# Longformer attention and a token and channel mixer on one core: interleaved queries for heads 4 to 7 of batch 0, mask rows behind adds, moved loads, and the last output tile in halves

## The chip, the cores and the metric

The kernel runs on one core of a Trainium2 chip. The metric is the device time of one execution in microseconds (us). Before the change the median of 5 runs is 309.93 us (307.6 to 310.61). All times below are in us from the start of the profiled span, unless they are durations.

## The reference, cut to what matters

For each of 8 batches and 8 heads, attention over 576 positions of 64 channels, with a mask: a query sees the keys within 32 positions, 8 global positions see and are seen by all. The result, as `x` of 576 x 512 per batch, goes through two dense layers along the positions and two along the channels.

```python
scores = scale * np.matmul(q, k.transpose(0, 1, 3, 2))
mask = np.abs(pos[:, None] - pos[None, :]) <= 32
mask = mask | is_global[:, None] | is_global[None, :]
attn = softmax(np.where(mask, scores, -1e9))          # along the keys
x = np.matmul(attn, v)                                # (8, 576, 512) after joining the heads
h = np.maximum(x.transpose(0, 2, 1) @ w_tok1, 0.0) @ w_tok2
u = x + h.transpose(0, 2, 1)
out = u + np.maximum(u @ w_ch1, 0.0) @ w_ch2
```

## The kernel before, in words

**Tiles.** A batch's 576 positions are five tiles (`tau`) of 128; the last holds 64. Only the band of the scores is computed. A head's band lies in the free dimension of `e_all` (`e0` for batch 0) in five blocks; the scores come as a "part 0" and a "part 1" for four heads (`hg`, 0 or 1), two heads to a PSUM tile.

**Work of one batch**, by the names in the profile:
- `load_qk`, `load_v`: loads on GpSimd's queue. `Xk`, `Xq`: transposes of k and q on VectorE (into `kc`, `qc`). `Kc`, `Xc`: GpSimd copies of these into `kT`, `qT`, where each tile's positions are interleaved with the 8 globals; `globals_`, `globals_k` (VectorE or GpSimd) write the globals there. `dup_v` is one copy `vsh<-vsh` on SP's queue, after the v loads.
- `S_step`: scores `s` of a `hg` and part; ScalarE takes the exponentials (L343). `S_mask`: VectorE multiplies a head's row of `e_all` by the band (L362), in pairs of heads 0, 1 and 2, 3 of the `hg`. `S_eg`: GpSimd copies the global columns into `eg`.
- `OG`: the rows of the global queries (`og`). `PV`: attention times v for a tile (`pv`), with two matmuls a head, and `norm` on VectorE.
- `M1` (`a1p`, then ScalarE), `M2` (`hp`, then VectorE adds `x` into `u`, and for the last 64 rows into `ul`), `M3`: SP's transposing DMA `uT<-u` (parts 0 and 1) and, in odd batches, `uTl<-ul`, since the last 64 rows of two batches are done together.
- `M4` (12 times: `b1p`, L492, then ScalarE), `M4l` (`b1lp`, L505, odd batches), `M5` (`op`, L518, four parts of three matmuls a tile; VectorE adds `u` into `osb`, L522 or L525; SP stores it).

**PSUM.** Pool `psm` has two one-bank buffers for `M4` and `M5`, `psS` two two-bank buffers (scores and others), `psV` one (all of `M2`, among others). A buffer is reused when its reader is done.

**Order.** Each round b of the loop merges two lists by their costs: first D4 (`M4` and `M4l` of batch b) with `OG`, `PV` and `M1` of batch b+1 and the transposes of batch b+2; then D5 (`M5` of batch b) with `M2` of b+1 and the scores of b+2. `run` calls a unit; `later(n, f)` calls f when n units, the present one among them, have run. So VectorE's queue has its masks after a fixed number of units (L562 to L569). Each engine runs its queue in order, and so do the DMA queues of GpSimd and SP. In a round D5 of even b, VectorE has: masks of heads 0, 1; masks of heads 2, 3; the `u` add of `M2` part 1; `osb`; `ul`; and for the second `hg`: masks 0, 1; `osb`; masks 2, 3; `osb`.

**Batch 0.** It is written out by hand (L730 on), heads 0 to 3 ahead of 4 to 7, in a buffer `e0` that lies where later `b1` and `wc2` do. Its scores (`S_nat`, L295) read the queries from `qc` and the globals apart, so that a segment is cut into pieces: 36 score matmuls a tile for part 0 and 32 for part 1, after the bias matmuls that add the mask (L298). `S_tile` (L315) does the same with 16 from the interleaved `qT`; batch 1 uses it. `fillt` issues matmuls on zeros that nobody reads.

Of the kernel before, what the change touches and what calls it, by code (L numbers as in the profile page):

```python
# [45 lines left out]
LAG_PV = 1  # L46
TDMA = 1
NEG = -20000.0
FILL = (33, 2, 0, 0)


@with_exitstack
def kernel(
# [31 lines left out]
    def pss(shape, dtype=F32, name="s"):  # L85
        return psS.tile(shape, dtype, tag="s", name=name)
# [93 lines left out]
    q16s = [halves(t) for t in qTs]  # L180
    qcs = [const.tile([P, NT * P], I32, name=f"qc{i}") for i in range(2)]
    kcs = [const.tile([P, NT * P], I32, name=f"kc{i}") for i in range(2)]
    e_all = const.tile([P, H, EW], F16)
    big = const.tile([P, 2, NJ, 512], F16)
    b1, wc2 = big[:, 0], big[:, 1]
    e0 = big.rearrange("p a j x -> p (a j x)")[:, 0 : H * EW].rearrange("p (h x) -> p h x", h=H)
# [125 lines left out]
                        )  # L312
        S_exp(b, hg, part, rp, ps)

    def S_tile(b, hg, part, rp, bias):  # L315
        ps = pss([P, 2, 512], name=f"s_{b}_{hg}_{part}_{rp}")
        qf, kT = q16s[b % 2][:, hg], k16s[b % 2][:, hg]
        if bias:
            for i in range(2):
                for off, c0, n in B_SEG[part]:  # L320
                    nc.tensor.matmul(
                        ps[:, i, off : off + n], lhsT=identS, rhs=biasm[:, c0 : c0 + n], start=(off == 0), stop=False,
                    )
        for off, kc, lo, n in S_SEG[part]:
            for e in range(2):
                for i in range(2):
                    r = 2 * rp + i
                    rs = slice(32 * r, 32 * r + 32)
                    nc.tensor.matmul(
                        ps[:, i, off : off + n], lhsT=kT[rs, kc : kc + P, e], rhs=qf[rs, lo : lo + n, e],  # L330
                        start=(e == 0 and not bias), stop=(e == 1 and (off == S_SEG[part][-1][0] or not bias)),
                    )
        S_exp(b, hg, part, rp, ps)
# [63 lines left out]
    def PV(b, tau, get):  # L397
        s = st[b]
        ps = get([P, 2, 512], name=f"pv_{b}_{tau}")
        odd_last = tau == NT - 1 and b % 2 == 1  # L400
        sh = 64 if odd_last else 0
        x16, vs = x16s[b % 2], vsh[b % 2]
        e = e_all if b else e0
        for hf in range(2):
            for hh in range(4):
                h = 4 * hf + hh
                o = ps[:, hf, VW * hh : VW * hh + VW]
                c0 = EB * tau + NG - sh
                m = 64 if tau == NT - 1 and not sh else P
                nc.tensor.matmul(o[0:m], lhsT=e[:, h, c0 : c0 + m], rhs=vs[:, tau, h, :], start=True, stop=(tau == NT - 1))  # L410
                if tau < NT - 1:
                    c1 = EB * tau + 136 + (NG if tau == 0 else 0)
                    nc.tensor.matmul(  # L413
                        o, lhsT=e[:, h, c1 : c1 + P], rhs=vs[:, NT - 1 + tau if tau else 1, h, :], start=False, stop=True
                    )

        def norm():
            r = slice(0, P) if tau < NT - 1 else slice(sh, sh + 64)
            pq = ps[:, :, 0 : 4 * VW].rearrange("p f (h x) -> p f h x", h=4)
            rr = tiny.tile([P, 2, 4], F32, tag="rr", name=f"rr_{b}_{tau}")  # L420
            nc.vector.reciprocal(out=rr[r], in_=pq[r, :, :, D])  # L421
            nc.vector.tensor_tensor(  # L422
                out=x16[r, tau, :].rearrange("p (f h x) -> p f h x", f=2, h=4), in0=pq[r, :, :, 0:D],
                in1=rr[r].unsqueeze(3).to_broadcast([P if tau < NT - 1 else 64, 2, 4, D]), op=ALU.mult,
            )
        return norm
# [83 lines left out]

    def M5(b, tau, part):
        s = st[b]
        if part == 0:
            s["o"] = psm([P, 512], name=f"op_{b}_{tau}")
        ps = s["o"]
# [45 lines left out]
    def u_S(b, hg, part):  # L561
        def f():  # L562
            S_step(b, hg, part)
            if part:
                later(LAG_S, lambda: S_mask(b, hg, (0, 1)))
                later(LAG_S + (5 if hg else 1), lambda: S_mask(b, hg, (2, 3)))
                later(LAG_S + (6 if hg else 2), lambda: S_eg(b, hg))
        return f

    def u_PV(b, tau, get):  # L570
# [327 lines left out]
    Xq(0, 1)  # L898
    Xv0(0)
    glob0(1)  # L900
    Xv0(1)
    S_nat(0, 0, 1, 0, psv, True)
    S_nat(0, 0, 1, 1, pss, True)
    load_v(0, (5, 6, 7), False)
    nc.gpsimd.dma_start(out=w1, in_=moe_w_tok1[0 : S - LAST, :].rearrange("(c p) x -> p c x", p=P))
    for i in range(2):
        nc.gpsimd.dma_start(out=w1l[64 * i : 64 * i + LAST, i], in_=moe_w_tok1[S - LAST : S, :])
# [6 lines left out]
    eg_const(1, nc.gpsimd.tensor_copy)  # L914
    nc.gpsimd.memset(vsh[1][32:64, NT:NC, :, 0:D], 0.0)
    load_v(1, (2, 3, 4), False)
    S_nat(0, 1, 0, 0, pss, True)
    S_nat(0, 1, 0, 1, psv, True)
    shift_v(0)
    nc.vector.memset(e0[:, 0:4, 200:208], 0.0)  # L920
    S_eg(0, 0)
# [9 lines left out]
    s0["uT"] = mb.tile([P, 4, 4, P], F16, tag="uT", name="uT_0")  # L931

    og = psm([P, 512], name="og0")
    OGh(0, og)
    S_nat(0, 1, 1, 0, pss, True)
    S_nat(0, 1, 1, 1, pss, True)
    zero_e(e_all)
    rfh(0, og)
    p01 = psv([P, 2, 512], name="pv0_01")
    fillt(p01[:, 1], FILL[2])  # L940
    PVh(0, PAIRS[0], p01)
    p23 = pss([P, 2, 512], name="pv0_23")
    PVh(0, PAIRS[1], p23)
# [109 lines left out]
    for b in range(B):  # L1053
        D4, D5 = dense(b)
        if b == 0:
# [21 lines left out]
            load_qk(3)  # L1077
            gather(gq, q, 1)
            gather(gk, k, 1)
            load_v(3)  # L1080
        else:
            A, Bs = [], []
            if b + 1 < B:
# [5 lines left out]
                A = G(b + 2) + A[:4] + weave(A[4:], X_units(b + 2))  # L1089
                Bs = mix(Bs, phase_s(b + 2))  # L1090
            if b + 3 < B:
                A = A[:2] + zero(lambda: load_qk(b + 3)) + A[2:]
                Bs = Bs[:5] + zero(lambda: load_v(b + 3)) + Bs[5:]
            merge(A, D4)
            merge(Bs, D5)
# [31 lines left out]
```

## Time and profile before

| | |
|---|---|
| median of 5 runs | 309.93 us |
| the 5 runs | 307.6, 309.93, 308.28, 309.98, 310.61 |
| the profiled execution | 308.04 us, of which the span is 306.2 |
| TensorE clock granted | 0.998 |
| idle before matmuls, all places | 13.4 (span less PE busy) |
| POOL waits for the masks, before `eg` copies (L368) | 66.9 in 12 places |
| SP waits for v loads, before `vsh<-vsh` (L130) | 99.2 in 8 places |
| round 0, D5 | about 57.4 to 73.6 |
| round 2, D5; round 4, D5 | about 126.5 to 142.2; 194.6 to 210.2 |
| scores of batch 3, first tile | 93.99 |
| last matmul starts, last add, last stores issued | 301.2, 301.58, 302.29 |

A timeline line holds the start, the duration, the engine, the line of the kernel, the operation with output and inputs, its shape, how many instructions are merged in it, and in brackets the idle time before it and what ended that. PE is TensorE's matmuls, PEld its weight loads, DVE VectorE, ACT ScalarE, POOL GpSimd, SP the queue that issues stores. A matmul of 512 columns has a duration of about 0.38 in its row, but they follow each other every 0.2155, since they are pipelined.

### The profile page before, as it was taken

To read this page: it belongs to the slowest core of one execution; us is meant where nothing else is said; L and a number is where in the kernel's file an instruction comes from. 1 tells how busy PE (TensorE), PEld (TensorE's weight loads), DVE (VectorE), ACT (ScalarE), POOL (GpSimd) and SP (SyncE) were. 2 spreads that over 40 slices of the span, in tenths; PEclk is the share of its full clock that TensorE was granted. 3 is DMA by queue.
4 is the path that set the end of the run, shared out by engine and by line. 5 is a ranking of instruction groups with operands and counts; after the bars stand their busy time and mean duration, and the time that the engine had idled before them with its cause. 6 is when DMAs were issued, how large, how long until landed. Compare 5 with 4: busy or idle time off the path is not lost.

```text
span 306.2 us, 8076 instructions
## 1 busy us (share of the span) xinstructions
PE 292.8 (96%) x3349; PEld 158.1 (52%) x3349; DVE 189.8 (62%) x369; ACT 156.9 (51%) x320; POOL 112.8 (37%) x212
## 2 busy tenths in 40 slices
PE   8998899899999999999999999999999999999993
PEld 3677565444565446444565446444564445444641
DVE  8877869785592767595582867585674865240021
ACT  7986795463545625654546524554455535206500
POOL 7898591332884560327140651326040000000000
PEclk9999999999999999999999999999999999999999
DMA  7999999996999699029941699049402320061022
GB/s 114 143 113 205 192 141 195 111 112 188 169 87 188 115 121 253 27 72 145 179 106 28 102 130 254 7 96 120 128 2 68 106 71 0 2 171 52 3 100 71
DMA packets 69381, 34.34 MB, mean 112 GB/s; under 512 B 55968, under 2 KB 59936, under 8 KB 69344
## 3 DMA queue, kind: packets, MB, share of 16 engines
q0 software_dynamic: 44960, 18.19, 50.6%
q1 hardware_dynamic: 24384, 15.63, 19.1%
q8 instruction: 26, 0.43, 0.6%
q14 instruction: 11, 0.09, 0.1%
HBM read 36.38 MB, written 9.44 MB: 150 GB/s over the span
## 4 chain that ended last, share of the span: by engine, by line
PE 63%; DVE 7%; POOL 3%; DMA 3%; issue 2%; ACT 1%; DVEq 0%; POOLq 0%; ACTq 0%
PE op L518 24%; PE b1p L492 20%; DVE e_all L362 5%; PE hp L451 4%; PE s L286 4%; PE a1p L435 4%; DMA q<-in_q_dram 3%; PE b1lp L505 3%; PE pv L410 2%; PE pv L413 2%; ACT e_all L343 1%; DVE u L456 1%; DVE osb L522 1%; POOL vsh L125 1%; PE og L378 1%
## 5 line engine op out<-in xcount | busy, mean ns | idle before, releaser
L719 ACT ACTIVATE big<-b1p 128x512 f16<-128x512 f32 x96 | 57.6, 602 | 79.1 <-PE b1p L492 79.1
L492 PE MATMUL b1p<-uT,wc 128*128 128x512 f16 x376 | 91.3, 379 | 1.5 <-DVE osb L522 1.5
L518 PE MATMUL op<-big 128*128 128x512 f16 x384 | 91.8, 380 | 0.0
L343 ACT ACTIVATE e_all<-s 128x544 f16<-128x544 f32 (+3 forms) x140 | 59.0, 522 | 32.5 <-PE s L286 30.6
L518 PEld LDWEIGHTS <-big 128*128 128x128 f16 x384 | 35.5, 98 | 40.5
L492 PEld LDWEIGHTS <-wc 128*128 128x128 f16 x376 | 33.5, 97 | 38.3 <-issue 4.8
L362 DVE TENSOR_TENSOR e_all<-e_all,bandm 128x1160 f16<-128x1160 f16 x54 | 38.1, 757 | 15.8 <-ACT e_all L343 15.8
L125 POOL DMA_DIRECT2D vsh<-in_v_dram x60 | 41.9, 711 | 3.7 <-DMA gq<-in_q_dram,idx_i 1.4
L456 DVE TENSOR_TENSOR u<-x,hp 128x1024 f16<-128x1024 f16 x14 | 17.0, 1217 | 31.8 <-PE hp L451 31.8
L522 DVE TENSOR_TENSOR osb<-u,op 128x512 f32<-128x512 f16 x32 | 21.9, 683 | 24.0 <-PE op L518 23.7
L368 POOL COPY eg<-e_all 128x160 f16<-128x160 f16 (+1 forms) x24 | 6.4, 295 | 66.9 <-DVE e_all L362 66.9
L253 POOL COPY kT<-kc 128x640 int32<-128x640 int32 x15 | 10.9, 724 | 48.1 <-DVE rr L421 35.0
L422 DVE TENSOR_TENSOR x<-pv,rr 128x512 f16<-128x512 f32 (+1 forms) x35 | 24.2, 691 | 1.4
L410 PEld LDWEIGHTS <-e_all 128*128 128x128 f16 (+1 forms) x280 | 17.9, 98 | 5.9 <-issue 1.5
L410 PE MATMUL pv<-vsh,e_all 128*128 128x66 f16 (+1 forms) x280 | 20.0, 194 | 0.2 <-DVE x L422 0.2
L451 PE MATMUL hp<-a,w 128*128 128x512 f16 x72 | 19.1, 379 | 0.8 <-DVE u L456 0.8
L240 DVE STREAM_TRANSPOSE kc<-k 128x576 int32<-128x576 int32 x16 | 19.9, 1243 | 0.1
L246 DVE STREAM_TRANSPOSE qc<-q 128x576 int32<-128x576 int32 x16 | 19.8, 1235 | 0.0
L286 PEld LDWEIGHTS <-kT 32*128 32x128 f16 x768 | 12.0, 92 | 11.3 <-issue 10.0
L413 PE MATMUL pv<-vsh,e_all 128*128 128x66 f16 x224 | 17.0, 193 | 0.1
L384 DVE TENSOR_TENSOR vsh<-og,dsel 32x132 f16<-32x132 f32 x28 | 8.1, 288 | 13.4 <-PE og L378 12.9
L286 PE MATMUL s<-qT,kT 32*128 32x104 f16 (+3 forms) x768 | 15.4, 214 | 1.0 <-POOL qT L253 0.6
(161 smaller groups left out, 323.6 us busy)
## 6 DMA issues: line engine op xcount, KB each, us to landing
out_dram<-osb SPq DMA_DIRECT2D x32, 256.0 KB, 2.4
k<-in_k_dram POOLq DMA_DIRECT2D x16, 288.0 KB, 5.9
q<-in_q_dram POOLq DMA_DIRECT2D x16, 288.0 KB, 8.3
vsh<-in_v_dram POOLq DMA_DIRECT2D x36, 96.0 KB, 5.4
vsh<-vsh SPq DMA_DIRECT2D x6, 297.0 KB, 5.8
wc<-in_moe_w_ch_dram POOLq DMA_DIRECT2D x3, 512.0 KB, 13.8
big<-in_moe_w_ch_dram POOLq DMA_DIRECT2D x3, 512.0 KB, 10.3
out_dram<-osb SPq DMA_DIRECT2D x8, 128.0 KB, 5.9
```

Of the source, the lines that this page charges most:

```text
L125: nc.gpsimd.dma_start(out=V[p0:p1, c, :, 0:D], in_=v[b, :, j0 : j0 + p1 - p0, :].rearrange("h p d -> p h d"))
L286: nc.tensor.matmul(tiles[r // 2][:, r % 2, off : off + n], lhsT=kT[rs, kc : kc + P, e], rhs=qf[rs, lo : lo + n, e], start=(e == 0), stop=( ...
L343: nc.scalar.activation(out=o, in_=i, func=AF.Exp, scale=scale)
L362: nc.vector.tensor_mul(out=eh, in0=eh, in1=bandm)
L410: nc.tensor.matmul(o[0:m], lhsT=e[:, h, c0 : c0 + m], rhs=vs[:, tau, h, :], start=True, stop=(tau == NT - 1))
L413: nc.tensor.matmul(o, lhsT=e[:, h, c1 : c1 + P], rhs=vs[:, NT - 1 + tau if tau else 1, h, :], start=False, stop=True)
L422: nc.vector.tensor_tensor(out=x16[r, tau, :].rearrange("p (f h x) -> p f h x", f=2, h=4), in0=pq[r, :, :, 0:D], in1=rr[r].unsqueeze(3).to_ ...
L451: nc.tensor.matmul(ps[:, i, :], lhsT=w2[:, ch, P * tau - sh : P * tau - sh + P], rhs=s["a1"][:, ch, :], start=(ch == 0), stop=(ch == 1),)
L492: nc.tensor.matmul(ps, lhsT=wc1[:, cc, P * j : P * j + P], rhs=s["uT"][:, :, cc, :], start=(cc == 0), stop=(cc == 3))
L518: nc.tensor.matmul(ps, lhsT=w, rhs=wc2[:, j, :], start=(j == 0), stop=(j == NJ - 1))
L522: nc.vector.tensor_add(out=osb, in0=s["u16"][:, tau], in1=ps)
L719: nc.scalar.activation(out=st[b]["b1"][:, j, :], in_=ps, func=AF.Relu)
```

## The change

1. **Start.** Heads 4 to 7 of batch 0 take their scores with `S_tile` instead of `S_nat`. For that `globals_` of these heads is done on VectorE and `Xc` on GpSimd, ahead of the weight loads. The tile of part 1, heads 4 and 5, moves ahead of `OGh(0)`; two fillers that write `og` stand between them.
2. **v of the last tile.** In even batches the last `pv` tile takes 128 columns of `e_all` where it took 64. The rows beyond are not read later. For the last head 64 columns are added behind `e_all` and zeroed on ScalarE.
3. **Masks.** The masks of heads 2, 3 and the `eg` copies come one unit later.
4. **Loads.** `load_v(3)` moves from the end of round 0 to round 1, behind the first two copies of globals for batch 3, where `load_qk(4)` stood; that one goes to the end of the first list.
5. **Last output tile.** Its `M5` is done in two halves of 256 columns, each in its own PSUM buffer, with its own add; the stores of the two batches' rows leave on SP's and ScalarE's queues.

```diff
-FILL = (33, 2, 0, 0)
+FILL = (33, 2, 2, 0)
...
-    e_all = const.tile([P, H, EW], F16)
+    e_pad = const.tile([P, H * EW + 64], F16, name="e_all")
+    e_all = e_pad[:, 0 : H * EW].rearrange("p (h x) -> p h x", h=H)
...
-    def S_tile(b, hg, part, rp, bias):
-        ps = pss([P, 2, 512], name=f"s_{b}_{hg}_{part}_{rp}")
+    def S_tile(b, hg, part, rp, bias, get=pss):
+        ps = get([P, 2, 512], name=f"s_{b}_{hg}_{part}_{rp}")
...
-                m = 64 if tau == NT - 1 and not sh else P
-                nc.tensor.matmul(o[0:m], lhsT=e[:, h, c0 : c0 + m], rhs=vs[:, tau, h, :], start=True, stop=(tau == NT - 1))
+                nc.tensor.matmul(o, lhsT=e_pad[:, EW * h + c0 : EW * h + c0 + P], rhs=vs[:, tau, h, :], start=True, stop=(tau == NT - 1))
...
+        if b == B - 1 and tau == NT - 1:
+            if part:
+                return
+            osb = ob.tile([P, DM], F32, tag="osb", name=f"osb_{b}_{tau}")
+            for c in range(2):
+                x = slice(256 * c, 256 * c + 256)
+                ps = psm([P, 256], name=f"op_{b}_{tau}_{c}")
+                for j in range(NJ):
+                    nc.tensor.matmul(ps, lhsT=s["b1l"][:, j, :], rhs=wc2[:, j, x], start=(j == 0), stop=(j == NJ - 1))
+                nc.vector.tensor_add(out=osb[:, x], in0=s["ul"][:, x], in1=ps)
+                for i, eng in enumerate((nc.sync, nc.scalar)):
+                    eng.dma_start(out=out[b - 1 + i, S - LAST : S, x], in_=osb[64 * i : 64 * i + 64, x])
+            return
...
-                later(LAG_S + (5 if hg else 1), lambda: S_mask(b, hg, (2, 3)))
-                later(LAG_S + (6 if hg else 2), lambda: S_eg(b, hg))
+                later(LAG_S + (6 if hg else 2), lambda: S_mask(b, hg, (2, 3)))
+                later(LAG_S + (7 if hg else 3), lambda: S_eg(b, hg))
...
     glob0(1)
+    globals_(0, nc.vector, (1,))
     Xv0(1)
...
     load_v(0, (5, 6, 7), False)
+    Xc(0, 1, nc.gpsimd)
     nc.gpsimd.dma_start(out=w1, in_=moe_w_tok1[0 : S - LAST, :].rearrange("(c p) x -> p c x", p=P))
...
-    S_nat(0, 1, 0, 0, pss, True)
-    S_nat(0, 1, 0, 1, psv, True)
+    S_tile(0, 1, 0, 0, True, pss)
+    S_tile(0, 1, 0, 1, True, psv)
...
     og = psm([P, 512], name="og0")
+    S_tile(0, 1, 1, 0, True, pss)
+    fillt(og, FILL[2])
     OGh(0, og)
-    S_nat(0, 1, 1, 0, pss, True)
-    S_nat(0, 1, 1, 1, pss, True)
+    S_tile(0, 1, 1, 1, True, pss)
     zero_e(e_all)
+    zeros(e_pad[:, H * EW :])
...
-    fillt(p01[:, 1], FILL[2])
...
-            load_v(3)
...
-                A = A[:2] + zero(lambda: load_qk(b + 3)) + A[2:]
+                if b == 1:
+                    A = A[:2] + zero(lambda: load_v(3)) + A[2:] + zero(lambda: load_qk(4))
+                else:
+                    A = A[:2] + zero(lambda: load_qk(b + 3)) + A[2:]
```

More of the change, by code (lines that the diff above doesn't have):

```diff
@@ L402, in PV @@
         x16, vs = x16s[b % 2], vsh[b % 2]
-        e = e_all if b else e0
+        e = e_all
         for hf in range(2):
```

## The prediction

> **What bounds the kernel now.** I read the page first, then TensorE's own waits, then the timeline at each place that the change touches.
>
> ```profile
> span 306.2 us, 8076 instructions
> PE 292.8 (96%) x3349; PEld 158.1 (52%) x3349; DVE 189.8 (62%) x369; ACT 156.9 (51%) x320; POOL 112.8 (37%) x212
> ```
>
> TensorE is busy 96% of the span and no other engine over 62%: only TensorE's 13.4 us of idle time, its own work, and the time after its last matmul can shrink. Its waits, with total, count and longest in us:
>
> ```profile
> PE b1p L492 <- DVE osb L522: 1.5, 3, 0.5
> ...
> PE a1p L660 <- DVE x L651: 0.9, 2, 0.7
> PE hp L451 <- DVE u L456: 0.8, 3, 0.3
> ...
> PE s L286 <- POOL qT L253: 0.6, 1, 0.6
> PE s L286 <- ACT a L438: 0.4, 1, 0.4
> ```
>
> Two come three times, in the dense second halves of rounds 0, 2 and 4. The timeline of round 0 (start, duration, engine, line) shows them; the other two rounds look alike:
>
> ```profile
> 66.29 1.47 PE L518 MATMUL op<-big 128*128 128x512 f16 x6
> 66.73 1.21 DVE L456 TENSOR_TENSOR u<-x,hp 128x1024 f16<-128x1024 f16 x1
> 68.00 0.59 PE L451 MATMUL hp<-a,w 128*128 128x512 f16 x2 [0.23 <-DVE u L456]
> 73.02 1.43 DVE L362 TENSOR_TENSOR e_all<-e_all,bandm 128x1160 f16<-128x1160 f16 x2
> 73.61 1.03 PE L492 MATMUL b1p<-uT,wc 128*128 128x512 f16 x4
> 74.36 0.68 DVE L522 TENSOR_TENSOR osb<-u,op 128x512 f32<-128x512 f16 x1
> 75.09 1.89 PE L492 MATMUL b1p<-uT,wc 128*128 128x512 f16 x8 [0.46 <-DVE osb L522]
> ```
>
> The adds that free a PSUM buffer stand behind two mask multiplies. One more place matters, the transpose of the odd batch's last rows (`uTl`) in round 2:
>
> ```profile
> 144.58 0.57 SPq L130 DMA_DIRECT2D vsh<-vsh  x1
> 145.24 2.36 SPq L470 DMA_TRANSPOSE uTl<-ul  x1
> ```
> ```profile
> 156.31 0.79 PEld L505 LDWEIGHTS <-wc 128*128 128x128 f16 x13 [0.26 <-DMA uTl<-ul]
> ```
>
> That transpose landed 11.0 us after its issue (the other measured ones 3.1 to 3.3), at 156.24; the matmul that reads it starts at 156.38, which is TensorE's natural time (155.51 + 4 x 0.2155 = 156.37). Its slack is nil.
>
> **Mask rows.** Between six-matmul groups and the next `hp` the odd round needs 1.30 us (102.81 to 104.11). In round 0 that makes 67.59, against 68.00: 0.41 lost; rounds 2 and 4 lose 0.47 each (134.81 to 136.58, 202.83 to 204.60). The second `b1p` group should follow 4 x 0.2155 = 0.86 after the first; it is 0.62, 0.69 and 0.69 late (75.09, 143.75, 211.77). With the masks of rows 2, 3 one unit later, the `u` add comes first and the last `osb` add starts when its matmuls end, some 73.39 in round 0; it ends at 74.07, and `b1p` goes on at 74.12 where 74.06 is natural. Gain 0.95 in round 0 and 1.1 in rounds 2 and 4. What is late next: the masks end 1.0 later, so GpSimd's `eg` copies end at about 76.1 for an `og` then due at 75.95, whose matmuls on the second copy come 0.36 after: covered by 0.2; uncovered it would cost those 0.1 to 0.2. In odd rounds TensorE does not wait here: nothing gained.
>
> But the first pair's `eg` is also 1.1 later (masks until 136.5 instead of 135.4), and on GpSimd's queue the loads of v stand behind it, on SP's queue the copy `vsh<-vsh` behind these, and `uTl` behind that. So in round 2 all of this chain, and the q and k loads behind the second `eg` that crowd it, move 0.8 to 1.1 later, while TensorE would come 1.1 earlier. `uTl` then lands near 157.2 and TensorE waits for it: round 2's gain is gone and 0.9 is lost. I take the 11.0 us landing again, since the q and k loads (issued 144.33 to 146.5) keep their distance to it. If it lands as the others do, in 3.1 to 3.3, nothing is lost; if it lands with the last q load (11.9 us after an issue at 145.94), 2.9. In rounds 0 and 4 the transposes have 14 and 7 us of cover (70.28 for 87.7, 213.94 + 3.1 for 224.4); without it they would cost the same way. Odd rounds: v loads 1.1 later, for an `og` 30 us off. Sum of rounds 0, 2, 4: -0.95 + 0.9 - 1.1.
>
> **Loads moved.** Scores of batch 3 start at 93.99 where TensorE was free at 92.62 + 0.65 = 93.27: they wait for GpSimd's copies, which stand behind eight v loads (82.4 to 89.5) and four q and k loads:
>
> ```profile
> 90.10 0.58 POOL L158 DMA_DIRECT2D k<-in_k_dram  x1
> 92.24 0.78 POOL L253 COPY kT<-kc 128x640 int32<-128x640 int32 x1
> 93.21 0.72 POOL L253 COPY qT<-qc 128x640 int32<-128x640 int32 x1
> 93.99 0.65 PE L286 MATMUL s<-qT,kT 32*128 32x136 f16 x32 [0.56 <-POOL qT L253]
> ```
>
> The four q and k loads of batch 4 (4 x 0.55 = 2.2 us of issue) go behind the copies; the eight v loads stay ahead of them, and the two copies of globals (0.76) go ahead of the v loads. The whole queue starts 1.1 later, since its first load stands behind the late `eg`. The globals' copies then fit into the 1.43 us that the v loads wait for a gather (at 86.25), about 0.6 less in the row. So the copies end at 93.93 - 2.2 + 1.1 - 0.6 = 92.2, and TensorE, 1.16 early, comes at 92.1. Gain 0.6; nothing if GpSimd's ring holds it longer, at most 0.72. The v loads land 0.8 later: the SP copy behind them went at 90.60 and SP's next item is at 98.22, so 6.8 us cover it. The q and k loads come 3.2 later, needed about 120: 15 us of cover.
>
> **Last v tile with all 128 columns.** The 128*64 form is dearer at both its ends: 0.95 from the first `b1p` matmul to it and 0.38 to the next (154.18, 155.13, 155.51), against 0.86 and 0.26 in the 128*128 form (120.67, 121.53, 121.79). 0.21 each in batches 2, 4, 6; that of batch 4 vanishes in the `uTl` wait. Gain 0.4, with nothing and 0.63 as ends.
>
> **Start.** A tile's scores take 36 or 32 matmuls in 0.70 or 0.66 us now (16.96 on, 20.86 on), and 16 in 0.46 in the interleaved form (45.39): 0.9 less of TensorE. But they must wait for a new GpSimd copy, 17.04 + 0.72 = 17.76, where they began at 16.96, and all of TensorE's queue waits behind them. ScalarE's exponentials run without a break from 13.36 to 20.42, 1.18 a tile, and would reach this tile at 18.06; its scores end near 18.45, so ScalarE loses 0.4. It then saves the 1.25 us gap at 21.68, because the seventh tile goes ahead of `og` (which waited for a v load until 20.19); the eighth follows `og`, behind two fillers (2 x 0.216). Exponentials end near 23.45 instead of 24.07. The next matmuls `a1p` gain that 0.6, but ScalarE must first zero `e_all` (1.40) and now the pad (0.25, near the 128x128 fill's 0.29), and its `vsh` writes gate the second half's `pv`: 25.1 for 25.40. I take 0.3. Ends: a gain of 1.25 (the whole gap) and a loss of 0.65 (0.4 + 0.25, nothing won back). The added DVE copy (0.22) is covered, since TensorE reaches `og` only at 20.7. The new copy puts the weight loads 0.72 later; v loads keep the DMA engines busy to 20.2 anyway, and `wc` had 4 us to spare.
>
> The row next to the new copy is GpSimd's copy at 14.64: 0.72, as long beside VectorE transposes as at 121.76. The Trainium skill's page "SBUF — State Buffer" says that VectorE's fast copies and GpSimd hold one shared port pair in turn, each for a whole instruction. The v shift at 17.66 is such a copy, 0.57 each; by that rule the new copy could end 0.57 later, the start would gain nothing, and the sum would be 2.95 instead of 3.25. No run here shows such a clash, so the sum goes by the row.
>
> **Tail.**
>
> ```profile
> 301.58 0.69 DVE L525 TENSOR_TENSOR osb<-ul,op 128x512 f32<-128x512 f16 x1 [1.90 <-PE op L518]
> 302.29 1.12 SPq L527 DMA_DIRECT2D out_dram<-osb  x2
> ```
>
> 24 matmuls of 256 columns take what 12 of 512 took (three take 0.49 at 29.81 and four 0.60 at 30.14, so 0.11 each against 0.2155: 0.05 more). The last add covers half the columns: 0.42 (the 64x256 row of L651), 0.27 less. The two last stores leave on two queues at once, so the second issue (0.5) goes. ScalarE is idle since 289.2. The landing, 2.3 us for 128 KB, 2.0 for 256 KB, does not shrink. Gain 0.8; ends 0.3 (only the add) and 1.2.
>
> **Sum** of the likeliest, in us: start -0.3, round 0 -0.95, scores of batch 3 -0.6, `uTl` +0.9, round 4 -1.1, v tiles -0.4, tail -0.8: -3.25. The profiled execution took 308.04 (span 306.2 and 1.84 around it), so 304.8 for one like it; the five runs lie between 307.6 and 310.61 with median 309.93, so 306.7 against the median.
>
> **Rivals.** (1) `uTl` is not held: it lands in time for the earlier TensorE. For: its 11 us is one event among crowded queues. Against: its whole chain moves later. Round 2 then gains 1.1 + 0.2 instead of losing 0.9: 5.45 in all, 304.5. (2) The front gives little: the start loses 0.6 (0.9 worse), batch 3's scores still wait (0.6 worse), the tail keeps only the saved issue (0.3 worse): 1.45 gained, 308.5. For: GpSimd's queue has 0.1 us of margin in two of these. Against: the rows as summed. (3) Slower: `uTl` starves behind the q and k loads. Each us past 157.2 costs one; with a landing 14.3 us after issue all is eaten, and with 16.5 the time is 312.2. For: two output stores beside it took 10.4. Against: nothing in the trace landed later than 14.8.
>
> **How the numbers follow.** Chances: forecast 0.48, (1) 0.22, (2) 0.23, (3) 0.07. The forecast's own range is 305.5 to 307.7. The range 304.2 to 309.2 takes in (1) and (2) and leaves out (3) and some edges, under 2 in 10. About 1%, 3.1 us, is what a measurement of this kernel can tell from no change; the forecast lies on that line, so half of it, and nearly all of (1), makes faster 0.47; the rest of it and (2) same 0.45; (3) and a little of (2) slower 0.08.
>
> **What would show it.** The waits of TensorE on `u` and `osb` are gone in rounds 0 and 4; batch 3's scores follow their matmuls with no wait on `qT`; the first `b1lp` of round 3 waits 1.5 to 2.5 us for `uTl`; no 128*64 form outside the start; ScalarE has a gap near 18 and none near 21; the last add is 256 wide and two queues store. I am wrong if `b1lp` shows no wait (then faster), if `a1p` starts later than 25.3, or if `og` waits for `eg`.

## The result and the profile after

| | before | after |
|---|---|---|
| median, all runs | 308.43 us (57 runs, 307.1 to 313.89) | 304.9 us (31 runs, 304.46 to 311.11) |
| ratio after to before, fast runs | | 0.9915, 95% interval 0.9892 to 0.9938 |
| profiled execution, span | 308.04, 306.2 | 305.72, 303.9 |

The forecast was 306.7 us, 3.25 less than the median then known; the profiled execution became 2.32 shorter, and the ratio means 2.6 less. The measured median, 304.9, lies below the range that the prediction gave as the forecast's own (305.5 to 307.7), although less was gained than forecast: the five runs that it started from had a median of 309.93, and 57 runs have 308.43. The granted clock differs between runs and chips (0.97 to 1.0 here), and the ratio leaves out the runs at the low clock that were over 1.5% above the fastest, so below times are compared at a clock of 0.998 or more, and effects under 1 us by stretches of the trace.

The page of the changed kernel: TensorE's share has risen, and ScalarE is 6.3 us busier (156.9 before), though the change adds no exponential and only one small fill. That is the first sign of something unforeseen.

```profile
span 303.9 us, 7874 instructions
...
PE 294.1 (97%) x3291; PEld 159.5 (52%) x3291; DVE 190.8 (63%) x371; ACT 163.2 (54%) x321; POOL 113.3 (37%) x213
```

TensorE's waits in it (total, count, longest): the two that came three times each, on `u` and on `osb`, are gone, and so is the one on `qT`. A new one is there, on `uTl`.

```profile
PE a1p L435 <- DVE x L422: 0.4, 1, 0.4
PE s L287 <- ACT a L438: 0.4, 1, 0.4
...
PE b1lp L505 <- DMA uTl<-ul: 0.2, 1, 0.2
```

Round 0 of the changed kernel's timeline, the place shown of before: the last `osb` add now stands ahead of the masks (75.02, then 75.62), and twelve `b1p` matmuls follow each other without a gap.

```profile
66.90 1.22 DVE L456 TENSOR_TENSOR u<-x,hp 128x1024 f16<-128x1024 f16 x1
68.04 1.43 DVE L363 TENSOR_TENSOR e_all<-e_all,bandm 128x1160 f16<-128x1160 f16 x2
...
69.04 0.59 PE L451 MATMUL hp<-a,w 128*128 128x512 f16 x2
...
74.98 2.76 PE L492 MATMUL b1p<-uT,wc 128*128 128x512 f16 x12
...
75.02 0.69 DVE L535 TENSOR_TENSOR osb<-u,op 128x512 f32<-128x512 f16 x1 [0.67 <-PE op L531]
75.62 1.43 DVE L363 TENSOR_TENSOR e_all<-e_all,bandm 128x1160 f16<-128x1160 f16 x2
```

Round 3, `uTl`: the weight loads of `b1lp` and then the matmul wait for it. The row of the `pv` group is now 128*128, 0.86 after four `b1p` matmuls begin at 153.33, with 0.26 to the next.

```profile
154.19 0.42 PE L410 MATMUL pv<-vsh,e_all 128*128 128x66 f16 x8
154.45 1.03 PE L492 MATMUL b1p<-uT,wc 128*128 128x512 f16 x4
155.72 1.07 PE L505 MATMUL b1lp<-uTl,wc 128*128 128x128 f16 x16 [0.24 <-DMA uTl<-ul]
```

The tail: two half adds, and stores leaving on two queues at once.

```profile
297.39 2.78 PE L521 MATMUL op<-big,b1l 128*128 128x256 f16 x24
...
298.90 0.42 DVE L522 TENSOR_TENSOR osb<-ul,op 128x256 f32<-128x256 f16 x1 [0.62 <-PE op L521]
299.35 1.78 SPq L524 DMA_DIRECT2D out_dram<-osb  x2
299.36 1.81 ACTq L524 DMA_DIRECT2D out_dram<-osb  x2
300.21 0.42 DVE L522 TENSOR_TENSOR osb<-ul,op 128x256 f32<-128x256 f16 x1 [0.89 <-PE op L521]
```

**Where the time went.** Cut both traces where a stage begins on TensorE, and take the stretches between. "Changed" is a second profile of the changed kernel (span 303.8), whose first exponential comes at 13.43 us, near the 13.36 of before; in the first profile it came at 14.04, since late gathers held the first scores. "Padded rows" is an experiment below. Names of rounds as in the kernel; `og` of batch b + 1 lies in round b.

| stretch, us | before | changed | padded rows | forecast of the change |
|---|---|---|---|---|
| first exponential to the `b1p` at 34.5 | 21.20 | 21.05 | 21.55 | -0.3 |
| from there to `op` of round 0 (batch 1's scores) | 22.82 | 23.76 | 22.82 | 0 |
| `op` of round 0 to `og` of batch 2 | 19.53 | 18.70 | 18.60 | -0.95 |
| that `og` to `op` of round 1 | 15.71 | 15.44 | 15.49 | -0.2 |
| `op` of round 1 to `og` of batch 3 | 20.31 | 19.91 | 19.68 | -0.6 |
| `op` of round 2 to `og` of batch 4 | 19.03 | 18.19 | 17.95 | -1.1 |
| that `og` to `op` of round 3 (with the `uTl` wait) | 15.69 | 16.47 | 16.63 | +2.0 |
| `op` of round 3 to `og` of batch 5 | 19.69 | 19.91 | 19.68 | 0 |
| `op` of round 4 to `og` of batch 6 | 19.02 | 18.19 | 17.95 | -1.1 |
| that `og` to `op` of round 5 | 15.70 | 15.43 | 15.47 | -0.2 |
| `op` of round 5 to `og` of batch 7 | 19.68 | 19.92 | 19.69 | 0 |
| last `op` tile to the end | 7.44 | 6.45 | 6.44 | -0.8 |

The changed column less that of before gives -2.40; three stretches of 13.61 that became 13.57 and the first exponential, 0.07 later, make it -2.45, the spans' difference (306.2 and 303.8). The gains are there nearly as forecast. But three stretches that the change was not thought to touch are longer: batch 1's scores by 0.94, and the odd rounds 3 and 5 by 0.22 and 0.24.

### The profile page after: what moved, and what is told of

Read it like the earlier page. It is cut to its first block, busy times and chain, and to the rows that moved or that the text cites. A ratio compares the mean times of both kernels' runs of the same rounds, so it can differ in the third digit from the quotient of the medians.

```text
span 303.9 us, 7874 instructions
## 1 busy us (share of the span) xinstructions
PE 294.1 (97%) x3291; PEld 159.5 (52%) x3291; DVE 190.8 (63%) x371; ACT 163.2 (54%) x321; POOL 113.3 (37%) x213
## 3 DMA queue, kind: packets, MB, share of 16 engines
q0 software_dynamic: 44960, 18.19, 50.9%
## 4 chain that ended last, share of the span: by engine, by line
PE 81%; DVE 5%; ACT 5%; DMA 5%; POOL 1%; issue 1%; DVEq 0%
PE op L531 30%; PE b1p L492 22%; PE hp L451 5%; PE s L287 5%; PE a1p L435 4%; PE b1lp L505 4%; DMA uTl<-ul 4%; ACT e_all L344 3%; PE pv L410 2%; DMA v<-in_v_dram 2%; PE pv L413 2%; DVE x L422 1%; PE og L379 1%; ACT big L732 1%; PE s L330 1%
## 5 line engine op out<-in xcount | busy, mean ns | idle before, releaser
L344 ACT ACTIVATE e_all<-s 128x544 f16<-128x544 f32 (+3 forms) x140 | 64.7, 503 | 28.2 <-PE s L287 25.3
L254 POOL COPY kT<-kc 128x640 int32<-128x640 int32 x15 | 10.9, 726 | 44.4 <-DVE rr L421 31.0
L410 PEld LDWEIGHTS <-e_all 128*128 128x128 f16 x280 | 18.1, 98 | 5.4 <-DVE x L422 0.7
L410 PE MATMUL pv<-vsh,e_all 128*128 128x66 f16 x280 | 20.0, 193 | 0.3 <-DVE x L422 0.3
L287 PEld LDWEIGHTS <-kT 32*128 32x128 f16 x768 | 12.4, 92 | 11.4 <-issue 9.4
L413 PE MATMUL pv<-vsh,e_all 128*128 128x66 f16 x224 | 17.1, 193 | 0.2 <-DVE vsh L389 0.2
L287 PE MATMUL s<-qT,kT 32*128 32x104 f16 (+3 forms) x768 | 16.7, 214 | 0.4 <-ACT a L438 0.4
L413 PEld LDWEIGHTS <-e_all 128*128 128x128 f16 x224 | 14.5, 97 | 3.0
## 6 DMA issues: line engine op xcount, KB each, us to landing
wc<-in_moe_w_ch_dram POOLq DMA_DIRECT2D x3, 512.0 KB, 10.6
```

The lines of the kernel that those rows point to most:

```text
L287: nc.tensor.matmul(tiles[r // 2][:, r % 2, off : off + n], lhsT=kT[rs, kc : kc + P, e], rhs=qf[rs, lo : lo + n, e], start=(e == 0), stop=( ...
L344: nc.scalar.activation(out=o, in_=i, func=AF.Exp, scale=scale)
L410: nc.tensor.matmul(o, lhsT=e_pad[:, EW * h + c0 : EW * h + c0 + P], rhs=vs[:, tau, h, :], start=True, stop=(tau == NT - 1))
L413: nc.tensor.matmul(o, lhsT=e[:, h, c1 : c1 + P], rhs=vs[:, NT - 1 + tau if tau else 1, h, :], start=False, stop=True)
```

## The experiments

The theories, as the expectations name them:
- **Theory A.** The flat tile costs time. Part 2 made `e_all` a slice of the flat `e_pad`. In the trace the second exponential of each tile of batch 1 then waits for the semaphore that ScalarE itself updates; with `e_all` a tile of its own it has no such wait from the second tile on. So the exponential starts only when the one before it has ended: in that second tile 0.03 after its end (39.55 and 39.52), with the padded rows 0.17 before it (39.04 and 39.21).
- **Rival B.** The tile's form is harmless, the slower exponentials have another cause.
- **Theory U.** `uTl` lands late because its transpose is issued late, behind the copy of v on SP's queue and so behind eight v loads, and then shares the DMA engines with four q and k loads. **Theory G.** On some chips round 1 loses time to GpSimd's gathers.

### The pad behind each head's row

```diff
-    e_pad = const.tile([P, H * EW + 64], F16, name="e_all")
-    e_all = e_pad[:, 0 : H * EW].rearrange("p (h x) -> p h x", h=H)
+    e_all = const.tile([P, H, EW + 64], F16)
...
-                nc.tensor.matmul(o, lhsT=e_pad[:, EW * h + c0 : EW * h + c0 + P], ...
+                nc.tensor.matmul(o, lhsT=e[:, h, c0 : c0 + P], ...
...
-    zeros(e_pad[:, H * EW :])
+    zeros(e_all[:, :, EW:])
```

> The changed kernel, but with the 64 zero columns behind each head's own row (a tile of 128 x 8 x 1224) in place of 64 columns behind a flat tile of which e_all is a slice. The last v tile still takes 128 columns. Theory A (the cost that the forecast missed is the flat tile: ScalarE's second exponential of each score tile then waits for ScalarE's first, so six exponentials of part 0 take 2.49 us instead of 2.22): the six take 2.2 again, batch 1's scores take about 11.4 from their first matmul to the last instead of 12.20, and the time is 0.8 to 1.1 us below the changed kernel's, near 304.7 for a profiled run or 0.989 of before. Rival B (the slower exponentials come from elsewhere, such as the moved start or the late gathers of that run, and the tile's form is harmless): the six stay at 2.5 and the time is the changed kernel's within 0.3.

Measured: median 306.56 (6 runs), ratio to before 0.9813 (0.9742 to 0.9885); this chip's runs of before at full clock took 309.60 and 309.68, more than elsewhere, so the time that the expectation gave for the changed kernel's chip cannot be read here. Batch 1's scores take 22.82 (35.07 to 57.89) as before the change, so theory A holds and B falls. (The expectation's 11.4 counts only up to the last score tile; the table's stretch goes on to `op`.) Beside the changed kernel itself on one chip:

> The changed kernel itself, to stand beside the three others on the same chip. On the two chips of the earlier experiments the kernel before took 309.5 at full clock, 2.5 more than its fastest runs elsewhere: ScalarE's first exponential came 1.0 later (14.3 to 14.4), and in round 1 og to b1lp took 11.7 to 12.8 instead of 10.6 to 10.8. If this chip is like these, some 307 to 307.5; if not, 304.5 to 305.7.

Measured: four runs at full clock took 304.45 to 305.56, before 308.26 to 308.49; ratio 0.9828 (0.9766 to 0.989). This chip was not like the two earlier ones.

> The kernel with the pad behind each head's own row once more, now beside the changed kernel. Theory A, with the terms read from the traces so far (flat tile: 0.96 in batch 1's scores, 0.22 in each of the odd rounds 1, 3 and 5, 0.1 to 0.2 in each of the even ones, about 2.0 in all; the larger pad's zeroing gives 0.4 back; the wait for uTl in round 3 grows by up to 0.7 since TensorE comes earlier): 0.9 to 1.6 us below the changed kernel, ratio to it 0.995 to 0.997. Rival B (the tile's form is harmless): within 0.3 of it.

Measured: ratio to before 0.9817 (0.9762 to 0.9872). The profiled spans are 302.6 and 303.8, 1.2 less, as theory A gave; the medians at full clock, 304.4 of five runs and 304.72 of the changed kernel's four, differ by 0.3 only. The changed kernel's profiled run (305.56) was its longest at full clock, and its `uTl` wait of 1.0 need not have come in the others; no trace shows them. So the time alone would not decide; the stretches do, and how it works is best read in round 3. The changed kernel:

```profile
170.25 2.50 ACT L344 ACTIVATE e_all<-s 128x544 f16<-128x544 f32 x6 [1.97 <-PE s L287]
...
172.56 0.85 PE L287 MATMUL s<-qT,kT 32*128 32x136 f16 x32
```

and the padded rows:

```profile
169.42 2.22 ACT L343 ACTIVATE e_all<-s 128x544 f16<-128x544 f32 x6 [2.18 <-PE s L286]
...
171.73 0.62 PE L286 MATMUL s<-qT,kT 32*128 32x136 f16 x32
```

Six exponentials take 2.50 instead of 2.22. The last pair of score tiles needs the two PSUM buffers that these free (its first matmuls wait for ScalarE's semaphore), so its matmuls stretch from 0.62 to 0.85: 0.23 of TensorE, and as much in four more rounds (0.10 in round 0). In batch 1 ScalarE frees the buffers of all eight tiles, hence 0.94. From the table, changed less padded rows: 0.94 + 0.10 + 0.23 + 0.24 + 0.23 + 0.24 + 0.23 = 2.21. The padded rows give back 0.5 in the start (the fills take 1.92 instead of 1.55, and a first tile that waits, see below), 0.16 in a longer `uTl` wait, 0.28 ahead of the first `b1lp` of round 7, whose cause I did not find, and about 0.2 in stretches where the flat tile is 0.04 or 0.05 shorter.

The groups by shape show how such a cost hides. Columns: busy time and mean ns of one, then idle time before them. Changed kernel:

```profile
L344 ACT ACTIVATE e_all<-s 128x416 f16<-128x416 f32 x28 | 14.5, 517 | 0.9
L344 ACT ACTIVATE e_all<-s 128x288 f16<-128x288 f32 x28 | 11.5, 410 | 0.9
```

Padded rows:

```profile
L343 ACT ACTIVATE e_all<-s 128x416 f16<-128x416 f32 x28 | 15.0, 534 | 0.0
L343 ACT ACTIVATE e_all<-s 128x288 f16<-128x288 f32 x28 | 12.0, 428 | 0.0
```

One exponential looks *shorter* in the changed kernel (517 against 534 ns), while six of them take longer: a record that overlaps its neighbour is longer, and the 0.9 of idle time ahead of the groups that follow in a tile (0.0 with the padded rows) shows that they no longer overlap. Mean durations of a pipelined engine do not give its rate; the length of a merged row does.

### The second part undone, and alone

```diff
-    e_pad = const.tile([P, H * EW + 64], F16, name="e_all")
-    e_all = e_pad[:, 0 : H * EW].rearrange("p (h x) -> p h x", h=H)
+    e_all = const.tile([P, H, EW], F16)
...
+                m = 64 if tau == NT - 1 and not sh else P
```

> The changed kernel without its second part: e_all a tile of its own, 64 columns in the last v tile of even batches. Theory A: exponentials at 2.2 for six, batch 1's scores in 11.4, so 0.8 to 1.1 won, against 0.4 to 0.6 lost at the 128*64 forms: 0.2 to 0.6 below the changed kernel, and 0.4 to 0.6 above the kernel with the padded rows. Rival B: 0.4 to 0.6 above the changed kernel, since only the 128 columns' gain is gone.

Measured: 305.66 (6 runs), ratio 0.9792 (0.9727 to 0.9857), beside 306.56 for the padded rows: four runs at full clock 305.45 to 305.68, against 305.28 to 306.93. Batch 1's scores 22.81. So undoing the part is no worse than padding the rows: the 128*64 forms cost no more than what the padded rows give back, which I had not counted. TensorE, which gains more in round 2 here, waits a full 1.06 for `uTl` in round 3:

```profile
159.36 0.44 PE L410 MATMUL pv<-vsh,e_all 128*64 128x66 f16 x8
159.73 1.04 PE L492 MATMUL b1p<-uT,wc 128*128 128x512 f16 x4
161.83 1.07 PE L505 MATMUL b1lp<-uTl,wc 128*128 128x128 f16 x16 [1.06 <-DMA uTl<-ul]
```

The second part alone, put into the kernel before:

```diff
-    e_all = const.tile([P, H, EW], F16)
+    e_pad = const.tile([P, H * EW + 64], F16, name="e_all")
+    e_all = e_pad[:, 0 : H * EW].rearrange("p (h x) -> p h x", h=H)
...
+                nc.tensor.matmul(o, lhsT=e_pad[:, EW * h + c0 : EW * h + c0 + P], rhs=vs[:, tau, h, :], start=True, stop=(tau == NT - 1))
...
+    zeros(e_pad[:, H * EW :])
```

> The kernel before with the second part alone (flat tile, 128 columns, zeroed pad). Theory A: 0.8 to 1.0 lost in batch 1's scores and something in the even rounds, 0.4 to 0.6 won at the v tiles: 0.1 to 0.5 slower than before, ratio 1.000 to 1.002. Rival B, and the forecast: 0.4 us faster, ratio 0.9987.

Measured: 313.97 (12 runs, few at full clock), ratio 1.0018 (0.9967 to 1.0069): the time tells nothing. The stretches do: batch 1's scores 23.77, `op` to `og` in rounds 0, 2 and 4 19.63, 19.19 and 19.20 (0.10, 0.16 and 0.18 more than before), in rounds 3 and 5 19.90 and 19.91 (0.21 and 0.23 more), and `og` to `op` of round 5 15.43, 0.27 less. That is a loss of 1.8. What is won shows in round 5 alone; in round 1 this chip's own loss hides it (see below), and round 3 is 0.19 longer, since it waits for `uTl`. Even with 0.27 won in all three rounds the part alone loses about 1 us by the stretches. Both the forecast (0.4 faster) and my 0.1 to 0.5 slower were too kind to it.

### Batch 0's exponentials in a tile of their own

```diff
-    e0 = big.rearrange("p a j x -> p (a j x)")[:, 0 : H * EW].rearrange("p (h x) -> p h x", h=H)
+    e0 = const.tile([P, H, EW], F16, name="e0")
```

(with the second part undone as above)

> The changed kernel without its second part, and batch 0's exponentials also in a tile of their own instead of a slice of the flat view of the buffer that later holds b1 and wc2. Theory A: the same wait of ScalarE for itself, present in both kernels in the start, goes too: six exponentials of the start take about 2.2 instead of 2.5, the row of eight tiles is about 1.0 shorter (9.5 from the first exponential to the last end instead of 10.54), and a1p comes 0.5 to 1.0 earlier: 0.5 to 1.0 us below the kernel without the second part. Rival B: the time of that kernel within 0.3, the start's exponentials unchanged.

Measured: 308.09 (8 runs), ratio 0.977 (0.9701 to 0.9839); four runs at full clock 305.21 to 306.04, no gain over 305.45 to 305.68. The start of both kernels was profiled under a lowered TensorE clock (0.60 and 0.58 between 16 and 31 us); ScalarE's exponentials do not show it: the first six took 2.50 in before, at 0.998. Part 2 undone:

```profile
14.31 2.49 ACT L343 ACTIVATE big<-s 128x544 f16<-128x544 f32 x6 [0.97 <-PE s L309]
16.99 1.17 ACT L343 ACTIVATE big<-s 128x544 f16<-128x544 f32 x2 [0.18 <-PE s L309]
```

and with `e0` its own tile:

```profile
14.29 2.22 ACT L343 ACTIVATE e<-s 128x544 f16<-128x544 f32 x6 [0.95 <-PE s L309]
16.82 1.03 ACT L343 ACTIVATE e<-s 128x544 f16<-128x544 f32 x2 [0.31 <-PE s L309]
```

The mechanism is theory A's, for a second tile: 2.49 to 2.22. The gain that I expected, 0.5 to 1.0, did not come: what ScalarE saves it waits for scores (0.31 for 0.18 here, and so on), and `a1p` comes 0.31 earlier. The lowered clock makes the scores later here; the kernel of "Together, and the gathers" shows the same at full clock.

### The first, third and fourth part alone, in the kernel before

```diff
+    globals_(0, nc.vector, (1,))
...
+    Xc(0, 1, nc.gpsimd)
...
+    S_tile(0, 1, 0, 0, True, pss)
+    S_tile(0, 1, 0, 1, True, psv)
...
+    S_tile(0, 1, 1, 0, True, pss)
+    fillt(og, FILL[2])
     OGh(0, og)
+    S_tile(0, 1, 1, 1, True, pss)
```

> The kernel before with the first part alone (interleaved queries for heads 4 to 7 of batch 0, the seventh score tile ahead of og, two fillers). The forecast: ScalarE's gap near 21 us is gone, and from ScalarE's first exponential to the b1p that begins batch 1's scores it takes 0.3 us less than before's 21.20, so 20.9. Reading of the changed kernel's trace (21.05 there, of which 0.15 is the pad's zeroing): 20.9 as well. Rival (start gives nothing, the row of exponentials is ScalarE's own work, 8 tiles of 1.17 to 1.30, and new gaps take the place of the old one): 21.1 to 21.3. Batch 1's scores, b1p to op, stay at 22.82, since e_all is a tile of its own here.

Measured: 313.58 (8 runs), ratio 0.9955 (0.9847 to 1.0063); at full clock 309.34 and 309.91, before 308.92 to 310.02 there. Inconclusive for the start: the profile fell into an execution whose granted clock was 0.50 from 16 to 25 us and 0.74 from there to 31. Batch 1's scores take 22.80, as expected without the flat tile.

```diff
-                later(LAG_S + (5 if hg else 1), lambda: S_mask(b, hg, (2, 3)))
-                later(LAG_S + (6 if hg else 2), lambda: S_eg(b, hg))
+                later(LAG_S + (6 if hg else 2), lambda: S_mask(b, hg, (2, 3)))
+                later(LAG_S + (7 if hg else 3), lambda: S_eg(b, hg))
```

> The kernel before with the third part alone (masks of rows 2, 3 and the eg copies one unit later). The forecast: waits of TensorE on u and osb gone; from the first op of rounds 0, 2, 4 to og 0.95, 1.1, 1.1 less than before's 19.53, 19.03, 19.02; then uTl makes the first b1lp of round 3 wait about 2.0, since the v loads and the uTl issue come 1.1 later. Theory A (the flat tile's slower exponentials stall score tiles in the even rounds, 0.2 to 0.3 each, so the changed kernel showed only 0.73, 0.86, 0.85): the full 0.95 to 1.1 here. Reading of the changed kernel on uTl (issued at the same time as before, because the uT transpose now goes ahead of the v loads on SP's queue; landing 10.7 later): the wait at b1lp is 0.4 to 0.8, not 2.0. In all 2.2 to 2.8 below before by the second theory, 1.1 to 1.5 by the forecast.

Measured: 307.54 and 309.66 (2 runs, at a clock of 0.996 and 0.987), ratio 0.9852 (0.972 to 0.9984), which two runs do not settle. `op` to `og` takes 18.60, 17.95 and 17.95: 0.93, 1.08 and 1.07 less than before, the forecast's 0.95, 1.1 and 1.1 to three hundredths. So the row arithmetic of that step was right, and the changed kernel's smaller gains are the flat tile's doing. The first `b1lp` of round 3 has no wait at all:

```profile
148.78 1.26 SPq L470 DMA_TRANSPOSE uTl<-ul  x1
...
159.11 1.06 PE L505 MATMUL b1lp<-uTl,wc 128*128 128x128 f16 x16
```

When this transpose landed is not recorded. Its packets tell it nearly (512 of 256 bytes): the last ended 5.1 after its issue, where in the ten other profiles with this order of the queue the last ended 9.4 to 10.9 after, and the landing was recorded at 9.9 to 11.6. Neither the forecast nor my second theory had that.

```diff
-            load_v(3)
...
+                if b == 1:
+                    A = A[:2] + zero(lambda: load_v(3)) + A[2:] + zero(lambda: load_qk(4))
+                else:
+                    A = A[:2] + zero(lambda: load_qk(b + 3)) + A[2:]
```

> The kernel before with the fourth part alone (v loads of batch 3 behind the globals' copies, q and k loads of batch 4 at the end of the list). The forecast: the wait of batch 3's scores for qT goes, from op of round 1 to the first score 1.37 becomes 0.74: 0.6 below before, or nothing if GpSimd's queue holds the copies as long as before, at most 0.72. Nothing else moves, since TensorE's later rounds have no wait on those loads.

Measured: 312.08 (8 runs), ratio 0.9958 (0.9878 to 1.0038). In the timeline of this kernel the scores follow `op` after 0.74, three matmuls of `op` and no wait, where before it took 1.37:

```profile
94.70 0.81 PE L518 MATMUL op<-big 128*128 128x512 f16 x3
...
94.86 0.56 POOL L158 DMA_DIRECT2D q<-in_q_dram  x1
95.40 0.55 POOL L158 DMA_DIRECT2D k<-in_k_dram  x1
...
95.44 0.64 PE L286 MATMUL s<-qT,kT 32*128 32x136 f16 x32
```

0.63 gained, as forecast; the loads of q and k now stand behind the copies and beside the scores.

### The transpose of `uTl` ahead of the copy of v

```diff
-                Bs = Bs[:5] + zero(lambda: load_v(b + 3)) + Bs[5:]
+                if b % 2:
+                    Bs = Bs[:5] + zero(lambda: load_v(b + 3)) + Bs[5:]
+                else:
+                    Bs = Bs[:5] + zero(lambda: load_v(b + 3, dup=False)) + Bs[5:6] + zero(lambda: dup_v(b + 3)) + Bs[6:]
```

> The changed kernel, but in rounds 2 and 4 the copy of v (vsh<-vsh) goes onto SP's queue behind the transpose uTl<-ul, which so no longer waits for the eight v loads. Theory U (uTl lands late because it is issued late and shares the DMA engines with four q and k loads): it is issued near 138 instead of 145, lands before 150, and b1lp of round 3 has no wait: 0.4 to 0.5 below the changed kernel from og to b1lp (10.96 becomes 10.55, as in round 1). Rival (something else holds that b1lp, or the copy of v that now comes later makes pv wait): no gain or a loss of up to 1.

Measured: 311.36 (8 runs, one at full clock: 306.6), ratio 0.9895 (0.9763 to 1.0027). SP's queue now has the transpose first; it lands 5.1 after its issue at most, and `og` to the first `b1lp` takes 10.56, against 10.96 and 11.58 in two profiles of the changed kernel. That much of theory U holds, and nothing waits for the later copy of v.

```profile
143.28 1.21 SPq L470 DMA_TRANSPOSE uTl<-ul  x1
150.29 0.56 SPq L130 DMA_DIRECT2D vsh<-vsh  x1
```

The run takes the transpose away from the copy of v and from the q and k loads at once. Round 4 tells the two apart. There the transpose follows the copy of v just as closely, in before:

```profile
213.27 0.57 SPq L130 DMA_DIRECT2D vsh<-vsh  x1
213.94 1.25 SPq L470 DMA_TRANSPOSE uTl<-ul  x1
```

But no q and k loads are issued beside it, and it lands in 3.0 to 3.2 in all eleven profiles with this order. So the copy of v alone does not make it late; the loads beside it remain as the cause, which no run moved by themselves.

### Together, and the gathers

```diff
+    e_all = const.tile([P, H, EW], F16)
+    e0 = const.tile([P, H, EW], F16, name="e0")
...
+        ef = e_all.rearrange("p h x -> p (h x)")
...
+                if tau == NT - 1 and not sh and h == H - 1:
+                    nc.tensor.matmul(o[0:64], lhsT=e[:, h, c0 : c0 + 64], ...
+                else:
+                    nc.tensor.matmul(o, lhsT=ef[:, EW * h + c0 : EW * h + c0 + P], ...
```

(in place of the changed kernel's lines, and with `uTl` first)

> The changed kernel with four edits that the experiments point to: e_all a tile of its own, whose last v tile reads 128 columns through a flat view for reading only (the last head keeps 64 columns, so no pad has to be zeroed); batch 0's exponentials in a tile of their own; the copy of v behind the transpose of uTl in rounds 2 and 4. Theory A and theory U: flat tile 2.0, uTl 0.4, start 0.3 to 1.0, no pad to zero 0.15, less 0.2 for the one 64-column matmul a batch: 2.5 to 3.3 us below the changed kernel. Rival B: only uTl's 0.4 and the pad's 0.15, so 0.5.

Measured: 305.54 (6 runs, two at full clock: 303.01 and 303.05), ratio to before 0.9846 (0.9784 to 0.9907). At full clock that is 1.7 below the changed kernel's median of 304.72 and 5.3 below before's 308.26 to 308.49; the profiled span is 301.2 against 303.8, 2.6 less. The profile is at the lower edge of what theories A and U gave, the timed runs are below it; no other version was faster by more than 0.1. Batch 1's scores 22.81, rounds 2 and 4 17.97, no wait for `uTl`. The start gives 0.19 only, of which 0.15 is the pad that is not zeroed, for the reason seen with `e0` (ScalarE waits 0.95 and 0.93 for scores where the padded rows have 0.61 and 0.59), and the 64-column matmul of the last head costs 0.27 and 0.26 in rounds 1 and 5 (15.71 and 15.69 for 15.44 and 15.43): one such matmul is as dear as eight.

```diff
-            gather(gq, q, 1)
-            gather(gk, k, 1)
...
+            merge(Bs[:5] + zero(lambda: (gather(gq, q, 1), gather(gk, k, 1))) + Bs[5:], D5)
```

> The same with one more edit: the four gathers of the second half's globals are issued in round 0 between the two eg copies, where GpSimd idles 7 us, and no longer at the start of round 1. Theory G (the 1.2 to 1.9 us that TensorE, VectorE and ScalarE lose in round 1 on the chips of the earlier experiments come from the gathers that GpSimd issues in just that stretch): on a chip that shows the loss it goes, 1.2 to 1.9 below the kernel best, and og to b1lp of round 1 takes 10.6. Rival (it has another cause, the q and k loads or the instruction stream): og to b1lp of round 1 stays at 11.7 to 12.8, time within 0.4 of best. On a chip without the loss both expect no difference.

Measured: 304.96 (6 runs), ratio 0.9816 (0.9754 to 0.9877); at full clock 302.97 to 303.96. Inconclusive for theory G: on this chip the changed kernel lost nothing in round 1 (`og` to `b1lp` 10.56), so there was nothing to win. The move cost something instead, which neither theory had: in its profile the `uT` transpose lands beside the gathers, and TensorE waits.

```profile
70.81 1.04 POOL L212 DMA_INDIRECT gq<-in_q_dram,idx_i  x1 [0.22 <-issue]
...
75.85 2.76 PE L495 MATMUL b1p<-uT,wc 128*128 128x512 f16 x12 [0.48 <-DMA uT<-u]
```

## Why the forecast came out near, step by step

The forecast's size is right partly because two errors cancel.

- **Mask rows**: right. Alone they give 0.93, 1.08 and 1.07; in the changed kernel 0.83, 0.84 and 0.83, because the flat tile stalls a score tile in each of these rounds. The forecast would be wrong "if `og` waits for `eg`": its weight loads do wait 0.4 in these rounds, but the matmuls do not, and 1.08 of 1.1 leaves no room for a cost.
- **`uTl`**: the wait came as forecast, the size did not. The prediction's "round 2's gain is gone and 0.9 is lost" would be +0.9 over the two stretches. The two profiles of the changed kernel show -0.71 and -0.06 (-0.84 + 0.78). The first `b1lp` of round 3 came 0.4 and 1.0 late, below the 1.5 to 2.5 named as the sign. The late landing came again (10.7 and 11.1), but the step failed where it moved "all of this chain" later: in the changed kernel the transposing DMA was issued at 144.98, 0.26 *earlier* than before. The v loads were issued 1.3 later, and the copy that waits for them still went at 144.32, where it had gone at 144.58. By putting `u` ahead of the masks the change also issued the `uT` transpose earlier (135.34 for 136.56) and so ahead of these loads; that this is why they land sooner was not tested.
- **Loads moved**: 0.63 for a forecast 0.6.
- **v of the last tile**: the two matmul rows were right, 0.27 for 0.21 a batch (0.22 with the padded rows). But the step costed the new tile at its rows on TensorE alone, and the form of the tile was the largest cost of the whole change, 2.2 us. The sentence that failed is the sum's "v tiles -0.4": with the flat tile it is about +1.4. It could have been read in the profile of before: there four exponentials of part 1 into `e0`, a slice of a flat view, take 2.39 (at 21.68), and four into `e_all`, a tile of its own, 1.96 (at 166.85). The forecast used the first rate, 1.18 a tile, and did not ask why it differs from the other.
- **Start**: 0.15 for a forecast 0.3, near. The gap near 21 us is gone, and there is one of 0.6 at 22.7, because the eighth tile stands behind `og` and two fillers. The forecast gap near 18 is there with the padded rows (0.61), but not in the two profiles of the changed kernel, whose exponentials run later in that stretch. In the first of these `a1p` starts at 25.83, past the 25.3 named as a sign of being wrong; that is the late first exponential, from which it is 11.79 instead of 11.95.
- **Tail**: 0.99 for a forecast 0.8. This part was not run alone, but nothing else of the change lies in that stretch.

Without the flat tile the change would have given some 4.6 by the stretches, the size of rival (1) less a little; with it 2.4. So the forecast's 3.25 is near by luck: the cost of the flat tile was left out, and the loss at `uTl` was put too high. Rival (1)'s time, 304.5, is closer still to the measured 304.9, and that is luck too: it counts a gain of 5.45 from 309.93, and TensorE does wait for `uTl`. Rivals (2) and (3) did not come: of the front only the start gave less, and `uTl` never landed later than 11.6 after its issue.

## What to carry to other kernels

When a change alters how a buffer is declared, cost every engine that writes it, not only the reader for which it was altered: look whether consecutive writes of one engine gained a wait on that engine itself. Where two tiles in one trace run the same instruction at different rates (2.39 and 1.96 for four), explain that before building on either. Of a chain that a step moves, follow each link's own wait: only the last to arrive sets the end.

## What the runs showed of the hardware that was not expected

- **ScalarE overlaps consecutive activations**, and a wait for its own semaphore between two of them costs some 0.14 (three exponentials take 1.17 without and 1.30 with one wait, two 1.03 and 1.17).
- **A port clash, in the start.** The prediction weighed what the Trainium skill's page "SBUF — State Buffer", section "Who interferes with whom", says of VectorE and GpSimd: one shared port pair, held by one of them for a whole instruction while the other blocks. No row that the prediction read showed it. The second profile of the changed kernel has VectorE's copy of globals beside GpSimd's new copy:

```profile
17.04 0.75 POOL L254 COPY qT<-qc 128x640 int32<-128x640 int32 x1
...
17.34 0.50 DVE L224 COPY qT<-gqT 128x80 f16<-128x80 f16 x1
...
20.51 0.37 DVE L224 COPY qT<-gqT 128x80 f16<-128x80 f16 x2
```

  The copy takes 0.50 where two of them take 0.37 later, and ends 0.05 after GpSimd's. In the kernel with the second part undone the same copy went ahead of GpSimd's (16.93, GpSimd's at 17.05) and took 0.19. That agrees with the page, though with the roles other than I had weighed them: GpSimd started first, and VectorE's copy was the one that took longer. The scores of heads 4 to 7 read both, and with the padded rows TensorE waits 0.84 for VectorE's. What it costs was not measured.
- **A loss in round 1 on two of the chips.** In all eight profiles from these two, of whatever kernel, `og` of batch 2 to the first `b1lp` takes 11.7 to 12.8 instead of 10.6 to 10.8; ScalarE, VectorE and then TensorE idle, in the stretch in which GpSimd issues the four gathers and just behind it. In the padded rows' first profile, with the gathers between 79.16 and 83.97:

```profile
84.98 1.08 ACT L731 ACTIVATE big<-b1p 128x512 f16<-128x512 f32 x2 [2.45 <-PE pv L412]
...
85.62 1.02 PE L491 MATMUL b1p<-uT,wc 128*128 128x512 f16 x4 [1.54 <-ACT big L731]
```

  There before mostly took 309.4 to 310.0 at full clock instead of 308.4 on the third. What it is stays open: moving the gathers was only tried on a chip without the loss.
- **The landing of `uTl`** in round 2, behind the copy of v and beside the q and k loads, was 9.9 to 11.6 in ten profiles; in an eleventh its packets ended after 5.1, with the same neighbours on the queues. What decides between the two was not found. Behind the copy of v without these loads it landed in 3.0 to 3.2, and ahead of both in 5.1 at most.
